# A new issue list for a fused attention and two mixture-of-experts kernel

## The chip, the core and the metric

The kernel runs on one core of a Trainium2 chip. Five instruction streams matter here: TensorE (PE in the profile, with its weight loads as PEld), VectorE (DVE), ScalarE (ACT), GpSimd (POOL) and SyncE (SP), which issues all DMAs. Each goes through its own list of instructions in order and waits on semaphores for what others produce. The metric is the device time of one execution in microseconds (us); lower is better.

## The reference

```python
# attention: batch 8, heads 8, seq 576, head_dim 64, 32 memory slots
a = softmax(phi, axis=seq)                    # per (b, h): 576 x 32
k_m = einsum('bhsm,bhsd->bhmd', a, k);  v_m = einsum('bhsm,bhsd->bhmd', a, v)
attn = softmax(q @ k_m.T / 8, axis=-1)        # 576 x 32
x = attn @ v_m                                # -> (4608 tokens, 512)
# first mixture: d_ff 768, the maximum of three products
h = maximum(maximum(x @ w1, x @ w2), x @ w3)
x = h @ w_out
# second, soft mixture: 8 experts with 4 slots each, F = 1024
logits = x @ phi2                             # 4608 x 32
d = softmax(logits, axis=0)                   # over all tokens
slot_in = d.T @ x                             # 32 x 512
for e in range(8):
    slot_out[e] = maximum(slot_in[e] @ W1[e], 0) @ W2[e]
c = softmax(logits, axis=1)
out = c @ slot_out
```

All of it is in fp32 in and out.

## The kernel before

The work is cut by batch entry n (8 of them, 576 tokens each) and, within it, by slices i (6 slices of 128 columns of the hidden 768). One pair (n, i) is a unit u; there are 48, and the first twelve mix n = 0 and n = 1. Since `x = attn @ v_m`, the product with `w1` to `w3` is folded: `v1` is `v_m` times the weights, and the expert matmuls multiply it by the attention matrix.

All of the main part up to a hand-over at the end is written as one string, `ORDER`: 1487 steps, separated by semicolons. A loop runs over it and calls the function that each step names (`for x in ORDER.split(";")`), so the order of steps in the string is the order of instructions on each engine. A step that stands later than another on the same engine never overtakes it. No scheduler moves anything afterwards. The code behind the loop, the tail, is written by hand: the last logits, the softmax over all tokens, the slots' experts (`ex_in`, L1016, takes the first weights), and the output.

The steps that the following speaks of, with the lines that the profile gives:

- `cva`, `cvb` (ACT), `cvd` (DVE, L318 and L319), `cvp` (POOL, L325) unpack weights; `raw`, `phit`, `phin`, `kv` and `q` are loads on SP. `send` (L286, L284) issues one piece of 512 KB of the second mixture's weights on SP, into a slot of memory that must be free. `late` opens further memory for these pieces (the tile `more`, and tiles that the earlier batch entries used).
- `warm` are filler matmuls (L801). `km`, `kvtm`, `scm`, `sct`, `s1r` to `s3t`, `s3h` and `s3l` (POOL, L532, writes `al`) make `k_m`, `v_m` and the attention matrix as a high part `ah` and a low part `al`.
- `v1m` (PE, L564), `v1h` (ACT, L573) and `v1l` (DVE, L579) make `v1` of a unit, in a high part `vh` and a low part `vl`.
- `mn u hf r` (PE, L597): six matmuls for unit u, half hf of its tokens and product r (0 to 2, for `w1` to `w3`), into one of three PSUM banks `m`. `ev u hf r` empties the bank: r = 0 is a copy on ACT (L607) into one of three buffers `g1`, r = 1 a maximum with it on DVE (L609), r = 2 the last maximum on DVE (L611) into the unit's tile `ht`. There are four `ht` buffers; a new unit's first L611 waits until all readers of the buffer's old unit are done.
- `ht` is read by `hrc` (POOL, L616), by `lg` (PE, L680, logits) and by a transpose. For n = 2 to 6, `trm` is a transpose on DVE (L643) into one of two half buffers and a DMA on SP out to memory (L645, `tr<-arena`); `trc` is a DMA on SP back in (L663, `hbuf<-tr`). For n = 7, `trm` is four transposes on PE (L639) and `trc` a copy on ACT (L659).
- `slm n k` (PE, L748) multiplies the transposed `hbuf` of three units by the softmax weights, after `ex`, `dtm` (PE, L733) and `dtc` (ACT, L737); `sla` (DVE, L760) adds it to the running sum.

The two steps at the heart, and the pools:

```python
ps_m = ctx.enter_context(tc.tile_pool(name="ps_m", bufs=3, space=PSUM))
gp = main_x.enter_context(tc.tile_pool(name="gp", bufs=3))
...
ht[n, i] = ring.tile([128, S], FP32, tag="ht", name="ht", bufs=4)
...
v = arena[:, o:o + 512]
nc.vector.transpose(out=v, in_=ht[n, i][:, 0:512])
...
nc.sync.dma_start(out=t, in_=v)
```

Of the kernel before, what the change touches and what calls it, by code (L numbers as in the profile page):

```python
# [22 lines left out]
for _x in (2, 3, 4, 5, 12, 6, 7, 13, 8, 9, 14, 15, 10, 11):  # L23
# [18 lines left out]
    "0 2; ev 1 1 0; raw 8; v1h 0 2; v1l 0 2; s1r 1 0; mn 1 0 0; cvp 7; ev 1 0 0; mn 1 0 2; cva 8; cvd 8; mn 1 0 "
    "1; ev 1 0 1; q 1 1; mn 2 0 0; raw 9; scm 1 1; ev 2 0 0; phi2; cvb 8; s1s 1 0; trm 0 0; trc 0 0; mn 2 1 0; ev "
    "1 0 2; s1e 1 0; sct 1 1; cvp 8; raw 11; mn 2 0 1; ev 2 1 0; hrc 0; mn 2 1 1; cva 9; cvb 9; raw 12; v1m 1 0; "
    "v1h 1 0; s2s 1 0; cvd 9; pt 0; pc 0; raw 10; ev 2 0 1; mn 2 0 2; ev 2 0 2; cvb 11; v1l 1 0; ev 2 1 1; mn 1 1 "
    "1; ev 1 1 1; mn 2 1 2; s2m 1 0; ev 2 1 2; phit 2; cva 11; cvp 9; raw 13; v1m 0 3; v1h 0 3; v1l 0 3; v1m 1 1; "
    "v1h 1 1; s3t 1 0; s3h 1 0; mn 1 1 2; ev 1 1 2; mn 4 0 0; ev 4 0 0; hrc 1; mn 4 1 0; ev 4 1 0; kv 2 0; cva "
    "10; mn 4 1 1; v1l 1 1; ev 4 1 1; mn 4 0 2; s1r 1 1; s3l 1 0; mn 3 0 0; ev 3 0 0; cvd 10; cvb 10; cvp 10; mn "
    "4 1 2; s1s 1 1; ev 4 1 2; cva 12; mn 4 0 1; ev 4 0 1; s1e 1 1; ev 4 0 2; pm 0; po 0; mn 5 0 0; s2s 1 1; mn 3 "
    "0 2; trm 0 1; hrc 4; trc 0 1; raw 14; cvd 11; cvp 11; pt 1; pc 1; mn 3 0 1; s2m 1 1; pt 2; pc 2; s3t 1 1; "  # L50
    "raw 15; s3h 1 1; s3l 1 1; ev 5 0 0; ev 3 0 1; ev 3 0 2; trm 0 2; phin 2; hrc 2; pm 1; po 1; cva 13; pm 2; lg "
    "0 0; cvb 12; cvd 12; cvp 12; lg 0 1; mn 3 1 0; ev 3 1 0; cva 14; mn 3 1 1; po 2; ev 3 1 1; cvb 14; mn 3 1 2; "
    "ev 3 1 2; hrc 3; cvb 13; mn 5 1 0; ev 5 1 0; trc 0 2; mxr 2; cvd 13; mn 5 1 1; trm 1 0; trc 1 0; mxd 2; mn 5 "
# [1127 lines left out]
```

## Time and profile before

| | |
|---|---|
| time, median of 3 runs (lowest to highest) | 465.71 us (465.19 to 467.65) |
| the profiled execution's own time | 465.06 us |
| its span in the trace | 463.3 us |
| mean granted clock of TensorE | 0.974 |
| busy, PE / DVE / ACT / POOL | 95% / 71% / 42% / 15% |

The time includes 1.8 us around the span. Busy is the share of the span in which an engine executes; a wait is the idle time in front of an instruction, put down to the one that released it. On a kernel whose PE is busy for 95%, it is PE's few idle stretches, and where they come from, that are worth reading.

### The profile page before, as it was taken

Reading aid. Unit: us, or ns where it says so; the run is one execution under the profiler, and the core shown is the slowest. Engines: PE = TensorE matmul, PEld = TensorE weight load, DVE = VectorE, ACT = ScalarE, POOL = GpSimd, SP = SyncE. Lnnn points to the kernel's source line nnn. Section 1 sums busy time; section 2 is a strip of 40 time slices with the busy share of each in tenths; the row PEclk is TensorE's granted clock in tenths of the full one; section 3 lists DMA queues with packets and bytes.
Section 4 is the critical chain, followed back from the end, with each engine's and each line's share of the span. In section 5 each row is a group of like instructions: output and inputs, shape, how many; then the busy total and the mean of one; then the engine's idle time right before and its main releaser. Section 6 shows DMA issues by size and latency. Waiting matters only on the chain.

```text
span 463.3 us, 12581 instructions
## 1 busy us (share of the span) xinstructions
PE 439.9 (95%) x5233; PEld 363.4 (78%) x5233; DVE 328.5 (71%) x753; ACT 192.6 (42%) x450; POOL 70.8 (15%) x92
## 2 busy tenths in 40 slices
PE   6999999999999999999999999998999989999981
PEld 5788899888997888888979879887878886654561
DVE  2397998767787968898679878999464434595541
ACT  3468768542544334243233433444333222133431
POOL 1137436421110011002100200112000000011000
PEclk9999999999999999999999999999999999999955
DMA  8967677558026137546368447779719905899988
GB/s 306 393 262 322 219 276 253 217 172 348 1 77 241 47 133 285 160 163 215 120 198 358 130 141 244 277 297 316 235 44 355 369 3 190 317 409 407 383 299 273
DMA packets 47657, 109.49 MB, mean 236 GB/s; under 512 B 3440, under 2 KB 26224, under 8 KB 45552
## 3 DMA queue, kind: packets, MB, share of 16 engines
q1 hardware_dynamic: 47600, 108.69, 64.8%
q8 instruction: 41, 0.67, 0.6%
q14 instruction: 16, 0.13, 0.1%
HBM read 91.38 MB, written 17.30 MB: 235 GB/s over the span
## 4 chain that ended last, share of the span: by engine, by line
PE 87%; DVE 4%; DMA 3%; ACT 2%; issue 1%; SPq 0%; DVEq 0%; ACTq 0%
PE m L597 49%; PE x L564 7%; PE l L801 5%; PE x L439 3%; PE x L1082 3%; PE x L748 2%; PE l L680 2%; PE x L475 2%; PE m L1016 2%; PE m L1033 2%; PE x L639 2%; DMA hbuf<-tr 2%; PE x L343 1%; PE l L1033 1%; DMA tr<-arena 1%
## 5 line engine op out<-in xcount | busy, mean ns | idle before, releaser
L597 PE MATMUL m<-ah,vh 128*128 128x288 f32 x576 | 171.2, 312 | 2.1 <-ACT g L607 1.5
L597 PE MATMUL m<-ah,vl 128*128 128x288 f32 x576 | 161.7, 296 | 0.0
L597 PEld LDWEIGHTS m<-ah,vh 128*128 128x128 f32 x576 | 108.3, 188 | 22.1 <-issue 9.4
L597 PE MATMUL m<-al,vh 128*128 128x288 f32 x576 | 123.3, 295 | 0.0
L597 PEld LDWEIGHTS m<-ah,vl 128*128 128x128 f32 x576 | 108.6, 188 | 0.2
L597 PEld LDWEIGHTS m<-al,vh 128*128 128x128 f32 x576 | 92.4, 188 | 0.1
L607 ACT ACTIVATE g<-m 128x288 f32<-128x288 f32 x96 | 38.9, 411 | 80.2 <-PE m L597 69.7
L609 DVE TENSOR_TENSOR g<-m,g 128x288 f32<-128x288 f32 x96 | 42.7, 450 | 33.0 <-PE m L597 22.4
L573 ACT ACTIVATE vh<-x 128x384 fp32r<-128x384 f32 (+1 forms) x100 | 42.0, 478 | 49.5 <-PE x L564 37.6
L611 DVE TENSOR_TENSOR ht<-m,g 128x288 f32<-128x288 f32 x96 | 42.7, 451 | 18.6 <-PE m L597 7.2
L579 DVE TENSOR_TENSOR vl<-x,vh 128x384 fp32r<-128x384 f32 (+1 forms) x100 | 48.8, 531 | 8.9 <-ACT vh L573 8.5
L532 POOL TENSOR_TENSOR al<-arena,ah 128x576 fp32r<-128x576 f32 x16 | 23.7, 1483 | 107.5 <-ACT ah L528 105.0
L564 PE MATMUL x<-arena,kvt 64*32 64x384 f32 (+1 forms) x800 | 39.3, 477 | 0.4 <-ACT vh L573 0.4
L325 POOL TENSOR_TENSOR arena<-arena 128x768 uint32<-128x768 uint32 (+1 forms) x13 | 23.4, 1804 | 39.5 <-ACT arena L313 14.5
L801 PE MATMUL l<-cst 128*128 128x128 f32 x162 | 25.3, 305 | 3.9 <-DMA cst<-in_consts_dram 3.2
L801 PEld LDWEIGHTS l<-cst 128*128 128x128 f32 x162 | 21.6, 208 | 7.3 <-DMA cst<-in_consts_dram 3.2
L564 PEld LDWEIGHTS x<-arena,kvt 64*32 64x32 f32 x800 | 12.0, 106 | 13.0 <-issue 8.1
L643 DVE STREAM_TRANSPOSE arena<-ht 128x512 f32<-128x512 f32 x30 | 20.7, 697 | 0.5 <-DMA tr<-arena 0.3
L439 PE MATMUL x<-arena 128*32 128x129 f32 x640 | 19.4, 274 | 0.2 <-ACT arena L402 0.2
L439 PEld LDWEIGHTS x<-arena 128*32 128x32 f32 x640 | 17.3, 110 | 2.9 <-ACT arena L402 0.9
L616 POOL COPY arena<-ht 128x64 f32<-128x64 f32 x24 | 5.2, 238 | 76.3 <-DVE ht L611 76.3
L528 ACT ACTIVATE ah<-arena 128x576 fp32r<-128x576 f32 x16 | 11.0, 684 | 11.2 <-DVE arena L518 11.2
(246 smaller groups left out, 587.3 us busy)
## 6 DMA issues: line engine op xcount, KB each, us to landing
arena<-in_e_w_dram SPq DMA_DIRECT2D x44, 512.0 KB, 7.5
arena<-in_w_dram SPq DMA_DIRECT2D x14, 768.0 KB, 6.0
arena<-in_kv_dram SPq DMA_DIRECT2D x8, 1290.0 KB, 9.5
arena<-in_q_dram SPq DMA_DIRECT2D x16, 576.0 KB, 7.0
arena<-in_kv_dram SPq DMA_DIRECT2D x8, 1032.0 KB, 8.1
tr<-arena SPq DMA_DIRECT2D x30, 256.0 KB, 3.0
hbuf<-tr SPq DMA_DIRECT2D x30, 256.0 KB, 4.3
arena<-in_phi_t_dram SPq DMA_DIRECT2D x8, 576.0 KB, 5.7
```

The costliest lines, as they stand in the source:

```text
L325: (eng or nc.gpsimd).tensor_tensor(out=du, in0=du, in1=lo.bitcast(U32), op=ALU.add)
L439: nc.tensor.matmul(t[32 * g:32 * g + 32, 0:KVC], phin_sb[:, j, b, 32 * g:32 * g + 32], kv_sb[:, j, b, g] if j < 4 else kv4_sb[:, g], start ...
L532: nc.gpsimd.tensor_tensor(out=al[n][:, :, c], in0=aT_sb[:, :, c], in1=ah[n][:, :, c].bitcast(FP32), op=ALU.subtract)
L564: nc.tensor.matmul(t[b][32 * g:32 * g + 32, 128 * r0:128 * r1], kvt[n][r, b, 32 * g:32 * g + 32], w_sb[r, i, r0:r1, g], start=True, stop=T ...
L573: nc.scalar.activation(out=v1[n, i][0][:, b, c], in_=ph["v1", n, i][b][:, c], func=ACTF.Copy)
L579: nc.vector.tensor_tensor(out=vl[:, b, c], in0=ph["v1", n, i][b][:, c], in1=vh[:, b, c].bitcast(FP32), op=ALU.subtract)
L597: nc.tensor.matmul(t[:, 0:HALF], x, y, start=(k == 0), stop=(k == 5))
L607: nc.scalar.activation(out=g1[u, hf], in_=t[:, 0:HALF], func=ACTF.Copy)
L609: nc.vector.tensor_tensor(out=g1[u, hf], in0=t[:, 0:HALF], in1=g1[u, hf], op=ALU.max)
L611: nc.vector.tensor_tensor(out=ht[n, i][:, cs], in0=t[:, 0:HALF], in1=g1.pop((u, hf)), op=ALU.max)
L643: nc.vector.transpose(out=v, in_=ht[n, i][:, 0:512])
L801: nc.tensor.matmul(t[:, 0:128], ident, ident, start=True, stop=True)
```

## The change

The string `ORDER` is replaced by another one. Its steps are the same ones, 1487 with the same arguments, the same 162 filler matmuls and the same 32 `send`; only their order differs, over its whole length. Nothing else in the kernel changes; the tail is the same code.

```diff
-    "dtc 6; slm 6 0; hrc 43; trc 7 4; sla 6 0; slm 6 1; sla 6 1; lg 7 1; ltm 0 3; hrc 40; trc 7 3; ev 47 1 2; ltc "
-    "0 3; lg 7 2; lg 7 3; lg 7 4; hrc 46; ev 47 0 2; hrc 47"
...
+    "1; hrc 46; mn 47 1 2; mn 47 0 2; ev 47 1 1; trm 7 2; trc 7 2; ltm 0 3; dtm 6; dtc 6; ev 47 0 2; trm 7 1; trc "
+    "6 3; trc 6 2; trm 7 4; trc 7 1; ev 47 1 2; trm 7 3; ltc 0 3; lg 7 1; slm 6 0; trc 7 3; slm 6 1; lg 7 2; lg 7 "
+    "3; trc 7 4; sla 6 0; sla 6 1; lg 7 4; hrc 47"
```

What that does to single engines is seen at three places. The first is SP's queue around the transfers that `slm 5 0` waits for. Here L645 is `tr<-arena` (out), L663 is `hbuf<-tr` (back in) and L286 a piece of weights. Before:

```order
L286 DMA arena<-in_e_w_dram 128x1024 x6
L645 DMA tr<-arena 128x512
L663 DMA hbuf<-tr 128x4x128
L645 DMA tr<-arena 128x512
L663 DMA hbuf<-tr 128x4x128
L286 DMA arena<-in_e_w_dram 128x1024 x3
L663 DMA hbuf<-tr 128x4x128 x3
L286 DMA arena<-in_e_w_dram 128x1024 x3
L645 DMA tr<-arena 128x512 x2
```

The two single L645 are `trm 5 5` and `trm 6 0`, and the five L663 in their order `trc 5 5`, `5 4`, `6 0`, `5 2` and `5 1`; three pieces stand directly ahead of the last three. In the new list:

```order
L286 DMA arena<-in_e_w_dram 128x1024 x4
L645 DMA tr<-arena 128x512 x2
L286 DMA arena<-in_e_w_dram 128x1024 x5
L645 DMA tr<-arena 128x512
L663 DMA hbuf<-tr 128x4x128 x3
L286 DMA arena<-in_e_w_dram 128x1024 x2
L645 DMA tr<-arena 128x512 x2
L286 DMA arena<-in_e_w_dram 128x1024 x3
```

In the new list `trc 5 2` and `trc 5 1` stand further up than these rows, and the three L663 here (`trc 5 4`, `5 0` and `5 5`) come directly behind the single L645 (`trm 6 0`) and ahead of the next pieces; `trc 5 0`, which stood further up before, is now the last that `slm 5 0` needs. The pieces stand in other groups as well.

The second place is ACT's last stretch ahead of the tail. L607 is `ev` with r = 0, L659 `trc` of n = 7, L737 `dtc 6`, and L794 `ltc`. Before:

```order
L573 ACTIVATE vh<-x 128x384 x2
L607 ACTIVATE g_5204<-m 128x288
L607 ACTIVATE g_5231<-m 128x288
L607 ACTIVATE g_5240<-m 128x288
L659 ACTIVATE hbuf<-x 128x4x4x32
L607 ACTIVATE g_5291<-m 128x288
L659 ACTIVATE hbuf<-x 128x4x4x32 x2
L607 ACTIVATE g_5356<-m 128x288
L737 ACTIVATE dk<-x 128x128
L659 ACTIVATE hbuf<-x 128x4x4x32 x2
L794 ACTIVATE hr_96<-x 128x384
```

In these rows L659 (`trc 7 0`, then `7 1` and `7 2`) stand between the L607; the last L607 comes behind three of them. In the new list:

```order
L573 ACTIVATE vh<-x 128x384 x2
L607 ACTIVATE g_5243<-m 128x288
L659 ACTIVATE hbuf<-x 128x4x4x32
L607 ACTIVATE g_5257<-m 128x288
L607 ACTIVATE g_5274<-m 128x288
L607 ACTIVATE g_5292<-m 128x288
L659 ACTIVATE hbuf<-x 128x4x4x32
L737 ACTIVATE dk<-x 128x128
L659 ACTIVATE hbuf<-x 128x4x4x32
L794 ACTIVATE hr_96<-x 128x384
L659 ACTIVATE hbuf<-x 128x4x4x32 x2
```

In the new list only `trc 7 0` stands among the L607; the other copies of n = 7 come behind the last of them.

The third place is DVE near unit 45 = (7, 3), in the same stretch. The numbers are those of buffers: a `ht` with a new number is a new unit's tile, L609 is `ev` with r = 1, L611 with r = 2. Before, `ht_5039` is unit 44 and `ht_5187` unit 45:

```order
L609 TENSOR_TENSOR g1_5059<-m_5173,g1_5059 128x288
L611 TENSOR_TENSOR ht_5039<-m_5154,g1_5059 128x288
L609 TENSOR_TENSOR g1_5188<-m_5196,g1_5188 128x288
L611 TENSOR_TENSOR ht_5187<-m_5206,g1_5188 128x288
L579 TENSOR_TENSOR vl_5193<-x_5122,vh_5192 128x384
L579 TENSOR_TENSOR vl_5193<-x_5123,vh_5192 128x384
L609 TENSOR_TENSOR g1_5240<-m_5251,g1_5240 128x288
L611 TENSOR_TENSOR ht_5187<-m_5213,g1_5240 128x288
```

In the new list `ht_4983` is unit 43, `ht_5155` unit 45 and `ht_5256` unit 46; `ht_4757` is unit 41 = (6, 5), and the L643 is its `trm 6 5`:

```order
L611 TENSOR_TENSOR ht_4983<-m_5180,g1_5078 128x288
L609 TENSOR_TENSOR g1_5172<-m_5190,g1_5172 128x288
L643 STREAM_TRANSPOSE arena_87<-ht_4757 128x512
L579 TENSOR_TENSOR vl_5210<-x_5082,vh_5209 128x384
L579 TENSOR_TENSOR vl_5210<-x_5083,vh_5209 128x384
L611 TENSOR_TENSOR ht_5155<-m_5215,g1_5172 128x288
L609 TENSOR_TENSOR g1_5156<-m_5223,g1_5156 128x288
L609 TENSOR_TENSOR g1_5257<-m_5235,g1_5257 128x288
L611 TENSOR_TENSOR ht_5155<-m_5260,g1_5156 128x288
L611 TENSOR_TENSOR ht_5256<-m_5277,g1_5257 128x288
```

In the list before, unit 45's tile takes the buffer of unit 42, which `trm 7 0` on PE reads. In the new list it takes the buffer of unit 41, which the L643 three rows ahead of its first L611 reads, and unit 46 takes that of unit 42.

## Rows read from the trace of the kernel before

**Rows 1.** page, part 1: busy us of each engine
```profile
PE 439.9 (95%) x5233; PEld 363.4 (78%) x5233; DVE 328.5 (71%) x753; ACT 192.6 (42%) x450; POOL 70.8 (15%) x92
```

**Rows 2.** windows: busy us of each engine, then granted clock, DMA share, GB/s
```profile
20.00:40.00 20.00, 19.41 (x226) 16.55 (x226) 18.45 (x38) 13.32 (x26) 8.62 (x6) 1.00 0.78 315
40.00:100.00 60.00, 59.75 (x672) 52.15 (x665) 50.34 (x102) 41.94 (x80) 30.05 (x22) 1.00 0.65 241
100.00:300.00 200.00, 199.93 (x2421) 171.36 (x2417) 163.92 (x375) 78.36 (x192) 19.58 (x37) 1.00 0.52 182
300.00:350.00 50.00, 48.27 (x577) 40.12 (x570) 36.16 (x85) 18.88 (x49) 5.47 (x9) 1.00 0.66 227
350.00:362.00 12.00, 12.00 (x116) 10.63 (x116) 5.51 (x14) 3.42 (x11) 0.65 (x3) 1.00 1.05 384
350.00:400.00 50.00, 47.11 (x489) 39.85 (x492) 22.23 (x56) 13.38 (x37) 1.72 (x8) 1.00 0.64 231
440.00:450.00 10.00, 8.39 (x71) 6.63 (x70) 4.59 (x13) 4.00 (x13) 0.00 (x0) 0.50 0.89 297
```

**Rows 3.** waits of PE, 300 to 390 us
```profile
PE x L748 <- DMA hbuf<-tr: 1.7, 1, 1.7
PE m L597 <- ACT g L607: 1.5, 2, 1.0
PE m L597 <- DVE ht L611: 0.6, 1, 0.6
```

**Rows 4.** chain that ended last, 312 to 325 us
```profile
312.45 3.29 DMA tr<-arena
...
317.19 7.58 DMA hbuf<-tr
...
324.86 0.85 PE x L748 x8
```

**Rows 5.** timeline of SP's queue, 313 to 318 us
```profile
313.72 1.36 SPq L286 DMA_DIRECT2D arena<-in_e_w_dram  x3
315.75 2.14 SPq L663 DMA_DIRECT2D hbuf<-tr  x3
```

**Rows 6.** page, part 6: DMA issues
```profile
hbuf<-tr SPq DMA_DIRECT2D x30, 256.0 KB, 4.3
```

**Rows 7.** timeline of DVE near 372 us
```profile
372.13 0.46 DVE L611 TENSOR_TENSOR ht<-m,g 128x288 f32<-128x288 f32 x1 [3.85 <-PE x L639]
```

**Rows 8.** timeline of PE, 371 and 383 us
```profile
371.50 0.60 PE L639 MATMUL x<-cst,ht 128*128 128x128 f32 x4
...
383.06 0.29 PE L597 MATMUL m<-ah,vh 128*128 128x288 f32 x1
...
383.85 0.27 PE L733 MATMUL x<-cst,dt 128*128 128x128 f32 x1
```

**Rows 9.** timeline of ACT, 381 us
```profile
381.20 0.60 ACT L659 ACTIVATE hbuf<-x 128x512 f32<-128x512 f32 x1 [0.63 <-PE x L639]
381.70 0.41 ACT L607 ACTIVATE g<-m 128x288 f32<-128x288 f32 x1
```

**Rows 10.** line L532 by itself: ns min/median/max
```profile
L532 POOL TENSOR_TENSOR al<-arena,ah x16: 1414/1437/2238, 31.6 to 322.3; 128x576 fp32r<-128x576 f32 x16
```

**Rows 11.** timeline of PE and SP, tail's start
```profile
399.69 1.07 PE L1016 MATMUL m<-extra,p 128*32 128x256 f32 x16
...
400.39 0.80 SPq L286 DMA_DIRECT2D extra<-in_e_w_dram  x2
```

**Rows 12.** timeline of SP's queue, 346 to 363 us
```profile
346.60 0.80 SPq L286 DMA_DIRECT2D more<-in_e_w_dram  x2
...
350.45 2.23 SPq L286 DMA_DIRECT2D arena<-in_e_w_dram  x3
...
355.51 0.93 SPq L645 DMA_DIRECT2D tr<-arena  x2
...
362.42 0.93 SPq L663 DMA_DIRECT2D hbuf<-tr  x2
```

253 rows, old and new, of the table ORDER are left out of this document.

## Prediction

> **What bounds the kernel now.** I read the page's busy times first. TensorE (PE) is busy 439.9 of 463.3 us, VectorE (DVE) 328.5 [rows 1], so the question is where PE stands idle and whether a new order can take that idle time away. The windows answer where [rows 2]: between 100 and 300 us PE is busy 199.93 of 200.00 us, between 40 and 100 us 59.75 of 60.00. There is nothing to win there, only something to lose. It is idle 0.59 us between 20 and 40 us, 1.73 us between 300 and 350, and 2.89 us between 350 and 400. The list that is searched anew ends at the hand-over to the tail, about 399 us; the code behind it stays.
>
> The waits of PE between 300 and 390 us come next [rows 3]. Three kinds are all there is: one wait of 1.7 us of a slot matmul (L748) for a transfer into `hbuf`, two waits of the expert matmuls (L597) for ACT's eviction `ev` with r=0 (L607), 1.5 us together, and one of 0.6 us for DVE's eviction with r=2 (L611). Together 3.8 us. These are the terms of the sum if the new order removes them.
>
> Where each comes from:
>
> The 1.7 us. The chain of waits [rows 4] goes from `tr<-arena`, issued at 312.45 and landed 3.29 us later, to a transfer `hbuf<-tr` issued at 317.19 that takes 7.58 us, and then to the eight matmuls of `slm 5 0` at 324.86. SP's timeline [rows 5] says why it took that long: three weight pieces (L286) are issued from 313.72, and only behind them, from 315.75, the three `hbuf<-tr`, of which the last is the one that `slm 5 0` needs. The median of this transfer is 4.3 us [rows 6], so 3.3 us of the 7.58 are crowding.
>
> The 0.6 us. DVE's timeline [rows 7] has an L611 at 372.13 after 3.85 us of waiting for a PE transpose (L639). It is `ev 45 1 2`; the buffer `ht` of unit 45 is that of unit 42, which `trm 7 0` reads, and PE comes to `trm 7 0` only at 371.50 [rows 8]. Until DVE goes on, PE's next matmul has no free `m` bank.
>
> The 1.5 us. ACT's timeline [rows 9] shows the larger of the two: an L607 at 381.70 (`ev 46 0 0`) stands behind a copy of PE's transposes (L659, `trc 7 2`) that waited 0.63 us for PE until 381.20. ACT goes through its list in order, so an eviction that was ready waits for a copy that nobody needs yet, and PE waits for the bank.
>
> **The change, part by part.** The steps are the same 1487, so no work is added or removed. Each engine's own list is all that changes, and each term is a wait.
>
> Slot matmul: `trc 5 2` and `trc 5 1` stand far earlier on SP, and `trc 5 0`, now the last that `slm 5 0` needs, comes directly behind `trm 6 0` and ahead of the next pieces. The three pieces that stood ahead were a wait of 2.0 us (313.72 to 315.75 [rows 5]), and the crowding was 3.3 us; five pieces ahead of `trm 6 0` may crowd in their place, but that stands some 5 us earlier against `slm 5 0` by the PE steps between. To lose the whole of 1.7 it is enough that the last transfer is issued 1.7 us earlier. I take the whole: -1.7 (bounds -1.7 and 0).
>
> ACT's copies: in the new order all L607 stand ahead of `trc 7 1` to `7 4`, only `trc 7 0` among them, so the pattern of [rows 9] is gone: -1.5 (bounds -1.5 and -0.5, if one of the two returns behind `trc 7 0`).
>
> DVE's buffer: unit 45's `ht` now reuses the buffer of unit 41, which is freed by DVE's own transpose `trm 6 5` (L643) directly ahead of it, and `trm 7 0` stands earlier on PE for the next unit: -0.6 (bounds -0.6 and 0).
>
> What may be given back at the end: evictions, transposes and copies are packed into the same stretch. DVE is busy 22.23 of 50 us and ACT 13.38 of 50 between 350 and 400 us [rows 2], so throughput is not short, only single orders. I take +0.3, a fifth of the 1.5 us that two such waits cost (bounds 0 and +1.0, the longest of them [rows 3]).
>
> Start, to 65 us: PE idles 0.59 + 0.25 us there [rows 2], so -0.8 is the most to gain. Against it, DVE is busy 18.45 of 20.00 us between 20 and 40 us with 38 instructions, 0.49 us each, and 50.34 of 60.00 behind that; two of them moved ahead of an eviction that PE needs cost 1.0 us. The new list swaps neighbours there and puts `mn 1 1 1` ahead of `mn 1 1 0`, so that its bank is held until both are evicted; counted step by step DVE's work and PE's come out level, 7.7 us each. I take 0 (bounds -0.8 and +1.0).
>
> A page speaks on one neighbour in that stretch. The row: `s3l 0 1` on GpSimd (POOL, L532) took 2238 ns where the median of 16 is 1437 [rows 10], 0.8 us more, and it lay across a DVE instruction with two SBUF inputs (L319). The Trainium skill, SBUF — State Buffer, section Who interferes with whom, says that such a DVE instruction and a GpSimd instruction that reads SBUF exclude each other for a whole instruction, whichever came first. The trace agrees with 0.8 us in one case of 16. By that rule the new order, in which `s3l 0 1` falls beside other DVE steps, could be up to 0.8 us better or worse for `al`; PE did not wait for it before, so the sum has 0 either way.
>
> Middle, 65 to 300 us: bounds 0 and +1.0 (one wait as long as the longest ACT wait at the end [rows 3]); the likeliest places are a DVE step that waits for a `phin` load, and a late `s3l`. I take 0.
>
> The tail: its first step, `ex_in(0)` (L1016), starts at 399.69, and the stream of weight pieces that fills the DMA queues follows at 400.39 [rows 11]. It hangs on buffers that PE's last steps free, so what the list saves shifts the whole tail.
>
> Sum, against the profiled execution's 465.06 us: 465.06 - 1.7 - 1.5 - 0.6 + 0.3 = 461.6. That execution lies 0.65 us below the median of the three runs (465.71), inside their spread of 465.19 to 467.65; by the median the sum is 462.2. I say **461.8**. With the bounds on all terms: 460.5 (-0.8 at the start, nothing given back) to 465 (below).
>
> **The rivals.** 0.5% is 2.33 us, about what a measurement of this kernel tells from no change: 463.38 to 468.04.
>
> (a) *The wait moves to `slm 6 0`.* The new order transposes `trm 6 5` late on DVE, behind `mn 45 0 1`, and issues its `tr<-arena` and then five `hbuf<-tr` in a row. Between `mn 45 0 1` and `slm 6 0` PE has 15 expert steps of 0.79 us (383.06 to 383.85) and five transposes of 0.60 us [rows 8], 14.9 us. DVE's eviction and transpose take about 1.4 us of it, 13.5 remain. The transfers need at best 3.3 us [rows 4], four issues of 0.7 us (2.14 for three [rows 5]), and 4.3 us [rows 6], 10.5 us; at worst 6.9 us, as `tr<-arena` issued from 355.51 was waited for until 362.42 [rows 12], 2.9 and 7.6 [rows 4], 17.4 us. So from 3.0 us of margin to 3.9 us of stall. Three weight pieces stand ahead of these transfers in the queue and none behind, so I hold the good half for likelier. With the stall, or with several of the bounds above at once (+1.0, +1.0, +0.7): 463.5 to 465.2.
>
> (b) *Slower: SP's queue stops DVE.* Once the list has opened more memory for weights, the new order issues ten pieces ahead of the `tr<-arena` of `trm 6 4` and `trm 6 3`, where before it was seven. Before, the first went out at 346.60, SP had to wait within the last three (2.23 us), and the two `tr<-arena` behind them, issued from 355.51, were waited for until 362.42 [rows 12], 15.8 us after the opening: the queues are full there, 1.05 busy at 384 GB/s [rows 2], so a piece of 512 KB takes 1.4 us. Now the opening comes 1.7 us earlier, at 344.9, three pieces more cost 4.2 us and two `hbuf<-tr` of half that size fewer give back 1.4: landed near 344.9 + 15.8 + 2.8 = 363.5. `trm 6 5` writes the half buffer that `trm 6 3`'s transfer reads, and it stands on DVE ahead of `v1l 7 4` and of evictions of units 45 to 47: if the transfer is late, DVE stands, no bank comes free and PE stands, 1:1. DVE wants it behind `mn 45 0 1`, 20 expert steps after the opening (15.8 us at 0.79 [rows 8]) and four `v1m` and three `lg`, some 3.5 us by my estimate: 364.7 with its eviction. The margin is 1.2 us, and 2.5 if a step takes 0.85 as it does behind a change of step; there it decides. To end 0.5% above before, the transfer would have to be 8 us later than counted: 468.1 or more. No transfer of this stretch shows such a delay, which speaks against it; a small overrun belongs to (a).
>
> (c) *The gain is hidden in the tail.* If the weight stream at 400.39 [rows 11] hung on something other than PE's last steps, the end would stay where it is and the list's gain would turn into waits for weights: 465.1. For it speaks that DMA is full in such stretches (1.05 [rows 2]); against it, that SP issues nothing new between 398 and 400 us and begins right behind L1016's start.
>
> (d) *More than the waits.* In the last part PE runs at half its clock: a granted clock of 0.50 between 440 and 450 us, 1.2 GHz, with 8.39 us of 10 busy, where it was 1.00 up to 400 [rows 2]. If the shifted tail kept the full clock longer, the queue of outputs, 0.89 busy there, would be the bound: about 1.1 us in these 10, 460.5 or a little less. Nothing in the tail's own order changes, which speaks against it.
>
> **The numbers.** Forecast 0.60 (own range 460.5 to 463.3), (a) 0.17, (c) 0.08, (b) 0.11, (d) 0.04. Faster by over 0.5%: the forecast and (d), 0.64. Within: (a) and (c), 0.25. Slower: (b), 0.11, which includes mishaps of that size that I did not find in a list of 1487 steps. The range leaves out (b) and the lower half of (d): 460.0 to 465.4.
>
> **What would show it.** Right: no PE wait over 0.3 us for `hbuf<-tr` at `slm 5 0`; no wait of L597 for L607 or L611 behind 365 us; `ex_in(0)` near 396.2 and the tail as long as before, 63.6 us from there to the span's end. Wrong: a PE wait at L748 near 380 (a), a DVE L643 with a long wait for `tr<-arena` near 365 (b), new PE waits between 40 and 300, or a longer tail with waits for weights (c).

## The result, and the profile after

The changed kernel takes 461.02 us (median of 4 runs, 459.66 to 462.82) against 465.67 for the kernel before (4 runs): the ratio is 0.9914, with a 95% interval of 0.9885 to 0.9942. The prediction was 461.8, in a range of 460.0 to 465.4. Run again in more rounds (e1 below) the ratio is 0.9878 (0.9848 to 0.9908). The ratios are those of the record, and not the quotients of the medians beside them (here 0.9900). One execution of e7 (469.45 us) was in a slower state and is left out of the table below. So the kernel is faster by about 1%, and the number was right. Its parts were not all right.

The profiled execution of the changed kernel is its slowest one: 462.82 us with a span of 461.0. Against the execution of before, 465.06, that is only 2.24 us less; the other 2.4 us are the distance of both traces from their medians (0.61 and 1.80). Its page, part 1, answers to [rows 1]:

```profile
PE 439.0 (95%) x5233; PEld 363.8 (79%) x5233; DVE 333.3 (72%) x753; ACT 192.4 (42%) x450; POOL 71.4 (15%) x92
```

And its windows (busy us of each engine, then granted clock, DMA share, GB/s) to [rows 2]:

```profile
20.00:40.00 20.00, 18.50 (x202) 16.24 (x186) 17.95 (x38) 12.47 (x24) 8.18 (x5) 1.00 0.89 348
40.00:100.00 60.00, 59.43 (x690) 51.00 (x692) 52.30 (x100) 42.14 (x81) 30.81 (x21) 1.00 0.55 209
100.00:300.00 200.00, 198.68 (x2345) 171.56 (x2334) 162.82 (x369) 77.56 (x191) 17.86 (x35) 1.00 0.54 186
300.00:350.00 50.00, 50.00 (x636) 41.07 (x634) 38.83 (x90) 19.74 (x51) 7.38 (x12) 1.00 0.59 203
350.00:400.00 50.00, 49.15 (x544) 42.10 (x544) 24.06 (x62) 13.88 (x38) 1.78 (x8) 1.00 0.77 282
```

Between 300 and 350 us PE now has no idle time, and between 350 and 400, where the tail begins 2.7 us earlier, 0.85 us. That is what was forecast. But between 20 and 40 us it is idle 1.50 us where it was 0.59, between 40 and 100 us 0.57 instead of 0.25, and between 100 and 300 us 1.32 instead of 0.07. The view of PE's waits names them (total us, times, longest):

```profile
PE x L564 <- DVE vl L579: 0.8, 1, 0.8
PE x L439 <- DMA arena<-in_kv_dram: 0.7, 1, 0.7
PE m L597 <- DVE ht L611: 0.6, 1, 0.6
PE m L597 <- ACT g L607: 0.5, 1, 0.5
PE x L564 <- ACT vh L573: 0.4, 1, 0.4
```

Two of these are of the kinds of [rows 3], but at other places. Between 300 and 390 us, where [rows 3] are from, the same view has none of the three: the waits for `hbuf<-tr`, for L607 and for L611 at the end are gone. New ones, 2.6 us together, stand at 29.71 (L579), 67.33 (L607), 132.18 (L611) and 260.29 us (a load of `kv`); the one of 0.4 us is the old list's too.

How the sum comes out: the list before comes to `slm 5 0` at 324.86 [rows 4] after a wait of 1.74, so without it at 323.1. The new list comes to it at 325.84 without a wait, with steps done that take PE 0.5 us more (`v1m 6 5` and an expert step, against an expert step and `rtm 0 1`). It has lost 2.2 us up to there. The first L1016 stands at 397.00, where it was 399.69 [rows 11]: from `slm 5 0` on, 71.16 us instead of 74.83, less the 0.5, a gain of 3.2 us. So the hand-over moves by 2.2 - 1.74 - 3.2 = -2.7 us, which is the -2.69 that the two rows give.

### The profile page after: what moved, and what is told of

Same layout as the page of the kernel before. It is cut to its first block, busy times and chain, and to the rows that moved or that the text cites. A ratio compares the mean times of both kernels' runs of the same rounds, so it can differ in the third digit from the quotient of the medians.

```text
span 461.0 us, 12577 instructions
## 1 busy us (share of the span) xinstructions
PE 439.0 (95%) x5233; PEld 363.8 (79%) x5233; DVE 333.3 (72%) x753; ACT 192.4 (42%) x450; POOL 71.4 (15%) x92
## 4 chain that ended last, share of the span: by engine, by line
PE 85%; DVE 5%; DMA 3%; issue 2%; ACT 2%; SPq 1%; POOL 1%; DVEq 0%; ACTq 0%; POOLq 0%
PE m L597 48%; PE x L564 7%; PE l L801 4%; PE x L439 3%; PE x L1082 3%; PE x L748 2%; DMA arena<-in_kv_dram 2%; PE x L475 2%; PE l L680 2%; PE m L1033 2%; PE m L1016 2%; PE x L639 2%; PE x L343 1%; PE l L1033 1%; SPq L663 1%
## 5 line engine op out<-in xcount | busy, mean ns | idle before, releaser
L597 PE MATMUL m<-ah,vh 128*128 128x288 f32 x576 | 171.4, 312 | 1.2 <-DVE ht L611 0.6
L597 PE MATMUL m<-ah,vl 128*128 128x288 f32 x576 | 161.8, 295 | 0.0
L597 PEld LDWEIGHTS m<-ah,vh 128*128 128x128 f32 x576 | 108.2, 188 | 20.6 <-issue 12.4
L597 PE MATMUL m<-al,vh 128*128 128x288 f32 x576 | 123.2, 295 | 0.1
L597 PEld LDWEIGHTS m<-ah,vl 128*128 128x128 f32 x576 | 108.4, 188 | 0.4
L597 PEld LDWEIGHTS m<-al,vh 128*128 128x128 f32 x576 | 92.3, 188 | 0.3 <-POOL al L532 0.3
L607 ACT ACTIVATE g<-m 128x288 f32<-128x288 f32 x96 | 38.9, 410 | 70.8 <-PE m L597 62.5
L609 DVE TENSOR_TENSOR g<-m,g 128x288 f32<-128x288 f32 x96 | 42.5, 449 | 31.0 <-PE m L597 24.4
L611 DVE TENSOR_TENSOR ht<-m,g 128x288 f32<-128x288 f32 x96 | 42.4, 450 | 20.3 <-PE m L597 9.0
L579 DVE TENSOR_TENSOR vl<-x,vh 128x384 fp32r<-128x384 f32 (+1 forms) x100 | 48.7, 530 | 3.3 <-ACT vh L573 2.8
L564 PE MATMUL x<-arena,kvt 64*32 64x384 f32 (+1 forms) x800 | 39.5, 477 | 1.3 <-DVE vl L579 0.8
L532 POOL TENSOR_TENSOR al<-arena,ah 128x576 fp32r<-128x576 f32 x16 | 23.3, 1465 | 72.1 <-ACT ah L528 42.5
L325 POOL TENSOR_TENSOR arena<-arena 128x768 uint32<-128x768 uint32 (+1 forms) x13 | 23.5, 1808 | 34.5 <-ACT arena L313 24.2
L801 PE MATMUL l<-cst 128*128 128x128 f32 x162 | 25.0, 303 | 3.8 <-DMA cst<-in_consts_dram 3.2
L801 PEld LDWEIGHTS l<-cst 128*128 128x128 f32 x162 | 21.6, 208 | 7.1 <-DMA cst<-in_consts_dram 3.2
L616 POOL COPY arena<-ht 128x64 f32<-128x64 f32 x24 | 6.3, 279 | 124.5 <-DVE ht L611 98.9
L564 PEld LDWEIGHTS x<-arena,kvt 64*32 64x32 f32 x800 | 12.4, 105 | 13.5 <-issue 7.8
L439 PE MATMUL x<-arena 128*32 128x129 f32 x640 | 19.8, 274 | 1.1 <-DMA arena<-in_kv_dram 0.7
L643 DVE STREAM_TRANSPOSE arena<-ht 128x512 f32<-128x512 f32 x30 | 20.5, 697 | 0.2
L439 PEld LDWEIGHTS x<-arena 128*32 128x32 f32 x640 | 17.3, 110 | 3.2 <-DMA arena<-in_kv_dram 0.9
L481 DVE STREAM_TRANSPOSE arena<-x 128x288 f32<-128x288 f32 x32 | 13.3, 457 | 3.7 <-PE x L475 3.7
```

Source lines behind the costliest of these rows:

```text
L325: (eng or nc.gpsimd).tensor_tensor(out=du, in0=du, in1=lo.bitcast(U32), op=ALU.add)
L439: nc.tensor.matmul(t[32 * g:32 * g + 32, 0:KVC], phin_sb[:, j, b, 32 * g:32 * g + 32], kv_sb[:, j, b, g] if j < 4 else kv4_sb[:, g], start ...
L532: nc.gpsimd.tensor_tensor(out=al[n][:, :, c], in0=aT_sb[:, :, c], in1=ah[n][:, :, c].bitcast(FP32), op=ALU.subtract)
L564: nc.tensor.matmul(t[b][32 * g:32 * g + 32, 128 * r0:128 * r1], kvt[n][r, b, 32 * g:32 * g + 32], w_sb[r, i, r0:r1, g], start=True, stop=T ...
L579: nc.vector.tensor_tensor(out=vl[:, b, c], in0=ph["v1", n, i][b][:, c], in1=vh[:, b, c].bitcast(FP32), op=ALU.subtract)
L597: nc.tensor.matmul(t[:, 0:HALF], x, y, start=(k == 0), stop=(k == 5))
```

## The experiments

The times, each beside the kernel before on the same chip, and the place of the first L1016 in the trace of each:

| kernel | us | before, us | ratio (95%) | L1016 at |
|---|---|---|---|---|
| e1 changed, again | 461.00 | 467.20 | 0.9878 (0.9848 to 0.9908) | 396.22 |
| e2 new from step 880 | 458.81 | 467.20 | 0.9839 (0.9804 to 0.9873) | 394.07 |
| e3 old from step 880 | 468.49 | 467.20 | 1.0033 (1.0004 to 1.0062) | 404.05 |
| e4 old to step 150 | 459.49 | 467.20 | 0.9864 (0.9824 to 0.9905) | 394.74 |
| e5 before, again, one run | 464.90 | 466.88 | | 400.81 |
| e6 SP's edit only | 464.54 | 466.88 | 0.9962 (0.9928 to 0.9996) | 403.29 |
| e7 the end by hand | 462.00 | 466.88 | 0.9907 (0.9876 to 0.9938) | 398.58 |
| e8 filler ahead of the wait | 459.83 | 466.88 | 0.9842 (0.9804 to 0.9880) | 394.51 |
| e9 three pieces ahead | 471.04 | 466.85 | 1.0097 (1.0071 to 1.0124) | 405.85 |
| e10 five steps by hand | 461.12 | 466.85 | 0.9871 (0.9845 to 0.9898) | 395.07 |
| e11 transpose early | 462.83 | 468.14 | 0.9897 (0.9856 to 0.9938) | 397.81 |
| e12 filler in e2 | 460.26 | 468.14 | 0.9863 (0.9813 to 0.9912) | 394.87 |

**e1, the changed kernel once more**, nothing edited.

> The changed kernel once more, nothing edited. Its first trace lost 1.7 us of PE time between 20 and 65 us against the kernel before, got back 2.0 us at slm 5 0 and 3.1 us behind 365 us. Theory A (the list costs time at the start): the waits at v1m (0.85 us near 29.7), at L597 near 67 us and 132 us come again at the same places, and the hand-over (first L1016) comes again near 397.0. Rival B (that trace was an unlucky execution): these waits are gone or elsewhere and the hand-over comes near 395.5. The time is 461.0 by either, ratio 0.990.

The waits of 0.42 and 0.85 us at the start, the one near 132 us and the one for `kv` (0.5) came again; the one near 67 us did not. The hand-over stands at 396.22, between what the two theories said. So the start's loss belongs to the list (A), and 0.8 us of the first trace were that execution's own.

**e2, e3 and e4, the two lists cut and joined.** Up to their steps 880 (before) and 879 (new) the two lists have done the same steps but one, near 230 us, and again nearly so near step 150. Each kernel takes one list to such a point and the other's order of what is left:

```diff
 # e2: ORDER[before][:880] + what is left, in the new order      (before's start and middle)
 # e3: ORDER[new][:879]    + what is left, in the order before   (new start and middle)
 # e4: ORDER[before][:150] + what is left, in the new order      (before's start)
```

> The list of before up to its step 880 (mxr 7, near 235 us), and from there the new list's order of what is left. Theory A: the start and the middle of before are kept, the gains of 2.0 and 3.1 us behind it are had, and the time is some 5 us below before and 1.5 to 2 us below the new list: 460.5 to 459.2. Rival B (start losses are not the list's): the same time as the new list, 461.0. Rival C (the end's gain needs what the new list did before): waits come back at slm 5 0 or behind 365 us, 463 or more.

> The other half: the new list up to the same point, and from there the order of before. Theory A: the three waits of before are back (1.7 at slm 5 0, 1.5 and 0.6 behind 365 us), and the start's loss of about 1.7 us comes on top: 467. Rival B: no loss at the start, the time of before, 465.7.

> The list of before up to its step 150 only (near 47 us), the new list's order from there. Theory A: if the loss is in the first 47 us, this wins it back and goes 1.0 to 1.7 us below the new list, 459.3 to 460.0; if it is between 47 and 65 us, where DVE's order decides, it stays at 461.0. Rival B: 461.0 in any case.

Theory A held in all three. e2 is the fastest kernel of the study, 2.2 us below e1 on the same chip; e3 is slower than the kernel before, by 0.3%; and e4, which takes only the first 150 steps from the old list, wins 1.5 us over e1 by the medians, so half or more of the loss lies ahead of 47 us. More cannot be said from e4: two of its six executions (462.3 and 462.5) lie above all of e1's, and its traced one was early already at the first L439 (14.84 us, and 15.26 in e2, which has the same steps up to there). Its trace has no wait of L564 for L579 (`v1l`) any more. In e3 the wait at `slm 5 0` is back, and longer, as its view of PE's waits shows:

```profile
PE x L748 <- DMA hbuf<-tr: 2.6, 1, 2.6
```

And in this trace the wait costs more than itself. It ends at 327.72, and from 329.1 to 332.5 us the granted clock is 0.50, as this window shows (the clock is the third figure from the end):

```profile
329.00:332.50 3.50, 3.50 (x28) 3.00 (x13) 1.02 (x2) 1.28 (x3) 0.00 (x0) 0.51 0.65 253
```

From `slm 5 0` to the first L1016 are 76.33 us, 1.5 more than in the first trace of before (74.83), which has the same order there and a clock of 1.00. In e5, below, a longer wait at the same place is not followed by a fall; what decides it, no run shows.

**e5, the kernel before once more**, one run.

> The kernel before once more, to see what its slower executions (up to 469 us, against 465.06 in the first trace) are made of. Theory: the wait at slm 5 0 hangs on when DMA data lands and is longer in them (2 to 4 us instead of 1.7), and the waits behind 365 us (0.50, 0.55, 0.99) are the same to 0.02 us. Rival: the time is lost in the tail, where the half clock and the weights decide; then the first L1016 stands near 399.7 again.

Its waits of PE between 300 and 390 us:

```profile
PE x L748 <- DMA hbuf<-tr: 3.2, 1, 3.2
PE m L597 <- ACT g L607: 1.5, 2, 1.0
PE m L597 <- DVE ht L611: 0.6, 1, 0.6
```

With the very same list the wait at `slm 5 0` is 3.2 us instead of 1.7, and those behind 365 us are the same to 0.01 us (0.50, 0.55, 0.99). So the wait that hangs on when data lands differs between executions, and the three that hang on the order of an engine's steps do not. The four traces that have this wait give 1.74, 3.22, 2.64 (e3) and 2.02 us (e7): the first was the shortest, and a prediction made against it expects too little of this term.

What the longer executions of before are made of, e5 does not show. They spread from 464.53 to 470.57 us on that chip, but the traced one was short: 464.90 us, with the longer wait and a hand-over 1.1 us later than in the first trace, since its tail took 62.3 us instead of 63.6. So the theory about them is not tested.

**e6, SP's part of the change alone.**

```diff
-  ...; hrc 32; rl 0 6; trc 5 2; trc 5 1; slm 5 0; ...
+  ...; mn 37 1 2; trc 5 2; trc 5 1; send 1; send 1; send 1; ...; hrc 32; rl 0 6; slm 5 0; ...
```

> The kernel before with one edit: trc 5 2 and trc 5 1 stand ahead of the three pieces (behind mn 37 1 2) instead of behind them. Theory: the wait of 1.7 us at slm 5 0 goes and the hand-over comes 1.7 to 2.0 us earlier, with the three waits behind 365 us unchanged: ratio 0.996. Rival: the pieces then come late or crowd a later transfer and the time is given back at slm 5 1 or slm 6 0: ratio 1.0.

The time fits the theory, the trace fits the rival. `slm 5 0` at 326.38 no longer waits, but 11 us later there is a wait in its place. In the timeline of DVE:

```profile
335.80 0.71 DVE L643 STREAM_TRANSPOSE arena<-ht 128x512 f32<-128x512 f32 x1 [2.57 <-DMA tr<-arena]
```

In that of PE:

```profile
337.47 0.30 PE L733 MATMUL x<-cst,dt 96*128 96x96 f32 x1 [1.69 <-ACT dt L719]
```

`trm 6 3` (L643) waits 2.57 us for the `tr<-arena` that reads its half buffer; DVE's steps for the softmax weights stand behind it, and PE waits 1.69 us for them. That transfer (of `trm 6 1`, the second of a pair on SP behind three pieces) is issued at 328.26, 1.9 us behind `slm 5 0`; in the list before it was issued at 324.60, 0.3 us ahead of it, while PE waited. The one wait had hidden the next. What is left of the gain, 0.4%, I put down to those executions in which that wait was longer than 1.7 us; that is argued from e5 and e3, not shown.

This traced execution also began 3.2 us late: the first L439 starts at 18.74 us instead of 15.55. It is not the first load, which landed 0.1 us later. The same fillers (L801) and transposes (L397) took about twice as long, as the chain shows, first before and then in e6:

```profile
9.72 1.17 PE l L801 x8
...
11.87 0.87 PE x L397 x8
```

```profile
10.15 2.09 PE l L801 x8
...
13.93 1.71 PE x L397 x8
```

The trace's first record of the granted clock, 1.00 (2.4 GHz), stands at 16.1 us in e6 and at 9.0 us in before; in the other traces it stands between 7.1 and 9.6 us. (The windows print 1.00 ahead of the first record too.)

**e7, the end by hand.** Two steps of the list before are moved.

```diff
-  ...; mn 45 1 2; mn 45 0 2; ...; v1l 7 4; trm 7 0; trc 7 0; ...
+  ...; mn 45 1 2; trm 7 0; mn 45 0 2; ...; v1l 7 4; trc 7 0; ...
-  ...; mn 46 0 1; trm 7 1; trc 7 1; mn 46 0 2; ...; trm 7 3; ev 46 0 0; ...
+  ...; mn 46 0 1; trm 7 1; ev 46 0 0; trc 7 1; mn 46 0 2; ...; trm 7 3; ...
```

> The kernel before with two edits at the end: trm 7 0 on PE directly behind mn 45 1 2 (for the ht buffer of unit 45), and ev 46 0 0 on ACT ahead of trc 7 1 and trc 7 2. Theory: both L607 waits (1.5 us) and the L611 wait (0.6 us) go, 2 to 3 us: ratio 0.994 to 0.996; the wait at slm 5 0 stays. Rival: ACT's or DVE's wait only moves on to the next eviction (unit 47), and half or less is won.

The theory held for the trace. From L748's start at 326.60 to L1016 at 398.58 are 71.98 us, 2.85 less than in the list before, and none of the three waits is left. Two steps out of 1487 bring most of what the new list brings at the end (3.2). It also shows that 2.04 us of idle time, by the rows, cost 2.85 us. A likely reason, not shown, is that a busy PE in these rows is not PE at its peak, as the profile's page says of its modelled ends. The ratio, 0.9907, is better than the 0.994 to 0.996 that were expected; where the rest of it comes from, the one trace does not show.

**e8, the start of the changed kernel.** One filler is moved.

```diff
-  ...; v1m 0 0 2 3; s3h 0 0; v1h 0 0 2 3; warm 8; warm 11; ...
+  ...; warm 8; v1m 0 0 2 3; s3h 0 0; v1h 0 0 2 3; warm 11; ...
```

> The changed kernel with one edit: the filler warm 8 stands ahead of v1m 0 0 2 3 instead of behind it. Theory: the new list lost 0.85 us near 29.7 us because PE waits there for v1l 0 0 1 2 with no filler ahead; with the filler ahead the wait goes and everything behind comes 0.85 us earlier, 460.2 against 461.0. Rival: DVE is the bound there, and the time comes back as waits behind 35 us: 461.0.

Its waits of PE between 20 and 300 us:

```profile
PE m L597 <- DVE ht L611: 0.6, 1, 0.6
PE x L564 <- ACT vh L573: 0.4, 1, 0.4
PE x L439 <- DMA arena<-in_kv_dram: 0.4, 1, 0.4
```

The wait for L579 (`v1l`) is gone, nothing came in its place, and the hand-over is 1.7 us earlier than in e1. Of these, 0.2 us were there ahead of the moved filler, and 1.2 arise at it (the first L597 stands at 33.47 us instead of 34.90); all six executions are below all of e1's, on another chip. PE's filler is work that has to be done in any case; behind the wait it is added to it, ahead of it it covers it.

**e9, three pieces ahead of `trm 6 4`** on SP.

```diff
-  ...; trm 6 4; ...; v1m 7 4; send 1; v1m 7 5; send 1; ...; send 1; ...
+  ...; send 1; send 1; send 1; trm 6 4; ...; v1m 7 4; v1m 7 5; ...
```

> The changed kernel with the three pieces that follow trc 6 4 put ahead of trm 6 4 and trm 6 3 on SP's queue (3 x 1.28 us). Theory (rival b of the prediction as a mechanism): in the new list tr<-arena of trm 6 3 landed 2.0 us before DVE wanted its half buffer for trm 6 5; with 3.8 us more DVE's L643 waits some 1.8 us, evictions stand behind it, and PE loses 1 to 1.8 us: 462 to 463 against 461.0. Rival: the banks and buffers in hand cover it: 461.0.

It does not test what it was meant to test. Pieces go into memory from which `v1m 7 4` and `v1m 7 5` still read their weights, and these steps now read pieces of another matrix: that part of the computation is changed. PE waits for a piece to land, as its timeline shows:

```profile
366.00 1.53 PE L564 MATMUL x<-arena,kvt 64*32 64x384 f32 x16 [8.30 <-DMA arena<-in_e_w_dram]
```

8.3 of the 10 us are this wait, not DVE's. For the rival it says nothing.

**e10, five steps by hand**: e6 and e7 together, and `trm 6 3` moved behind `rdc`, so that the wait that e6 showed goes too.

```diff
-  ...; ev 39 1 2; trm 6 3; mn 40 0 0; ...; rtm 1 0; rdc; rsm 0; ...
+  ...; ev 39 1 2; mn 40 0 0; ...; rtm 1 0; rdc; trm 6 3; rsm 0; ...
```

> The kernel before with all edits by hand: trc 5 2 and 5 1 ahead of the three pieces, trm 6 3 behind rdc (the wait that appeared in its place), trm 7 0 behind mn 45 1 2, ev 46 0 0 ahead of trc 7 1. Theory: five moved steps hold the new list's whole gain, without its start: 5 us below before and below the changed kernel by 1 to 2 us, 459 to 460 against 461.0. Rival: the searched list's many other moves are needed and a part of the waits comes back: 462 or more.

None of the three waits is left, nor the one of e6, and L1016 stands at 395.07, 1.15 us ahead of e1. The time is the changed kernel's, not 1 to 2 us less: its tail took 63.93 us in that trace (62.78 in e1), since its last two groups of L1033 took 1.18 and 2.02 us where the others took 1.00: the weights' stream, of which more is said below. Five moved steps hold what the new list gained; that they are better than it is not shown.

**e11, the transpose early**: the rival (b) as a mechanism.

```diff
-  ...; ev 45 0 0; v1l 7 5; ev 43 0 2; ...; mn 45 0 1; ev 45 0 1; trm 6 5; trc 6 5; ...
+  ...; ev 45 0 0; trm 6 5; trc 6 5; v1l 7 5; ev 43 0 2; ...; mn 45 0 1; ev 45 0 1; ...
```

> The changed kernel with trm 6 5 (and its trc 6 5) ahead of v1l 7 5 on DVE, four evictions earlier. Theory (rival b as a mechanism, with a dependence that the three pieces of the run before did not keep): in e1 the tr<-arena of trm 6 3 landed at 365.84 and DVE would now want the half buffer at 363.8, so its L643 waits 2.1 us, v1l 7 5 and four evictions stand behind it, and PE waits 1 to 2 us for banks near 366: 462 to 463 against 461.0. Rival: three banks and DVE's idle time of 1.5 us behind cover it: 461.0.

In DVE's timeline:

```profile
365.33 0.71 DVE L643 STREAM_TRANSPOSE arena<-ht 128x512 f32<-128x512 f32 x1 [1.85 <-DMA tr<-arena]
```

In PE's:

```profile
367.37 0.40 PE L597 MATMUL m<-ah,vh 128*128 128x288 f32 x1 [1.68 <-DVE ht L611]
```

The theory held to 0.3 us: DVE waits 1.85 us for `tr<-arena`, PE 1.68 for the eviction that stands behind, and the kernel takes 462.83 (e1: 461.00, on another chip; L1016 1.59 us later, and 1.9 us counted from `slm 5 0`). The mechanism of the rival is real; in the new list it was not reached.

**e12, the rule of e8 put into e2.**

```diff
-  ...; v1m 0 0 2 3; v1h 0 0 2 3; phit 1; s1s 0 0; cvd 1; s1r 0 1; s1e 0 0; warm 4; ...
+  ...; warm 4; v1m 0 0 2 3; v1h 0 0 2 3; phit 1; s1s 0 0; cvd 1; s1r 0 1; s1e 0 0; ...
```

> e2 (before up to step 880, the new order from there) with the filler warm 4 ahead of v1m 0 0 2 3 in the part of before, where PE waited 0.42 us for ACT. Theory: the best of both lists and the start's rule of e8: 0.4 us below e2, 458.4, 1.9% below before. Rival: no difference from e2, 458.8.

Its waits of PE between 20 and 100 us:

```profile
PE m L597 <- POOL al L532: 0.7, 1, 0.7
PE m L597 <- ACT ah L528: 0.7, 1, 0.7
```

A miss. The wait of 0.4 us for ACT goes, but ACT's `s3h` and POOL's `s3l` come 2.2 us later than in e2, and the first expert steps wait 0.7 us for each of them. 460.26 is no gain over e2. A part of the 2.2 us is the moved filler: `v1h 0 0 2 3` and the steps behind it on ACT and DVE come about half a us later. The larger part is one DVE instruction, `s2m 0 0` (L514), which takes 2.40 us where the other 15 take 0.75. DVE's timeline:

```profile
29.15 2.40 DVE L514 TENSOR_TENSOR arena<-arena,ssum 128x576 f32<-128x576 f32 x1
```

POOL's:

```profile
28.78 2.16 POOL L325 TENSOR_TENSOR arena<-arena 128x768 uint32<-128x768 uint32 x1 [2.73 <-ACT arena L313]
```

L514 has two SBUF inputs and started 0.4 us behind POOL's L325. In e2 it ran at 28.60, and POOL's L325 began behind it, at 29.44. So e12 does not refute the rule of e8; it shows that a moved filler also changes which instructions of DVE and POOL meet. `s3h` waits for DVE's L518, which stands behind L514.

## Why the prediction was right, and where not

The number is in part luck. Up to `slm 5 0` the new list lost 2.2 us where the sum has 0, and behind it it won 3.2 us where the sum has 1.8, so two errors cancel in part. What was right is which waits go, and in the main why.

*The three waits go.* Right in all: behind 300 us no row of them is left. The terms were -1.7, -1.5 and -0.6, with +0.3 given back. Mis-sized are two. The end measured -3.2 (e7: -2.85 with two steps) instead of -1.8: nothing was given back, and in e7 the waits cost PE more than their idle rows say. The slot matmul is -1.7 in the traced pair, but 3.2 in e5.

*The reading of [rows 5].* The three pieces are not all that held back the three `hbuf<-tr`. SP had issued the pieces by 315.08 (313.72 + 1.36). The first of the three L663 is `trc 6 0`, which needs the `tr<-arena` of `trm 6 0`, landed at 315.74 (312.45 + 3.29 [rows 4]), and the queue went on at 315.75; the pieces crowd these transfers. In e5 that `tr<-arena` landed at 318.58, the three went out from 318.60, and PE waited 3.2 us. e6 moved the two L663 ahead of the pieces and of `trc 6 0` alike, so it does not part the two causes.

*ACT's and DVE's places.* In the new trace's timeline of ACT the evictions L607 stand ahead of the copies L659 as in the order shown, and each waits for PE, not PE for it:

```profile
374.47 0.41 ACT L607 ACTIVATE g<-m 128x288 f32<-128x288 f32 x1 [1.19 <-PE m L597]
376.04 0.41 ACT L607 ACTIVATE g<-m 128x288 f32<-128x288 f32 x1 [1.17 <-PE m L597]
381.35 0.60 ACT L659 ACTIVATE hbuf<-x 128x512 f32<-128x512 f32 x1 [4.90 <-PE x L639]
```

In DVE's timeline `trm 6 5` and the first L611 of unit 45 start without a wait:

```profile
368.89 0.70 DVE L643 STREAM_TRANSPOSE arena<-ht 128x512 f32<-128x512 f32 x1
...
370.43 0.44 DVE L611 TENSOR_TENSOR ht<-m,g 128x288 f32<-128x288 f32 x1
```

*`slm 5 0` has 5 us.* Wrong in the margin. SP's timeline of the changed kernel:

```profile
318.16 0.33 SPq L645 DMA_DIRECT2D tr<-arena  x1
318.54 1.57 SPq L663 DMA_DIRECT2D hbuf<-tr  x3
```

And PE's:

```profile
325.84 0.51 PE L748 MATMUL x<-hbuf,dk 128*32 128x384 f32 x1
```

`trc 5 0` is issued 0.5 us behind the first L663, 319.0, and landed at 324.2; the last of the three, landed at 325.0, is `trc 5 5`, which `slm 5 0` does not need. PE came at 325.84. So the transfer took 5.2 us where the median is 4.3 [rows 6]: it was crowded, as the prediction allowed, and 1.6 us were left.

*Start: 0, bounds -0.8 and +1.0.* This step failed. "Counted step by step DVE's work and PE's come out level": between 45 and 65 us neither trace of the new list has a wait, but the loss lies ahead of that, at a place that the count passed over. PE's `v1m 0 0 2 3` stands ahead of its filler in the new list and waits for DVE there. e4 gives 1.5 us for the first 150 steps by the medians, and 1.1 by the hand-over without that early start (396.22 - 394.74 - 0.42); in e8 1.2 us arise at the one filler. So the term was at its upper bound or somewhat beyond, where 0 was taken.

*Middle: 0, bounds 0 and +1.0.* At its upper bound or beyond: one wait of 0.57 near 132 us and one of 0.5 to 0.7 for a load of `kv` came in both traces, 1.1 to 1.2 us together, and in the first one of 0.5 near 67 us besides. Neither of the two places that were named (a `phin` load, a late `s3l`) was among them.

*Rival (a), `slm 6 0`.* Said: from 3.0 us of margin to 3.9 of stall. SP's timeline:

```profile
366.28 0.37 SPq L663 DMA_DIRECT2D hbuf<-tr  x1
...
374.98 2.58 SPq L663 DMA_DIRECT2D hbuf<-tr  x5
```

And PE's:

```profile
383.27 1.47 PE L748 MATMUL x<-hbuf,dk 128*32 128x384 f32 x16
```

Five `hbuf<-tr` are issued from 374.98, the last landed at 382.24, and `slm 6 0` starts at 383.27 without a wait: a margin of 1.0 us.

*Rival (b), SP's queue.* Said: `tr<-arena` landed near 363.5, a margin of 1.2 to 2.5 us. The L663 that waits for the first of the two goes out at 366.28 (above), the second landed at 366.9, and DVE's L643 started without a wait at 368.89: 2.0 us. The times on the clock came about 3 us later than counted, most of it the 2.2 us lost ahead of 326; the margin was right, and e11 shows what lies behind it.

*Rival (d), the clock.* The clock did stay high longer in some traces of the new list, but e5 shows that the list need not be the cause. The window from 438 to 440 us of the changed kernel, with the granted clock third from the end:

```profile
438.00:440.00 2.00, 1.46 (x13) 1.15 (x13) 1.07 (x4) 0.97 (x4) 0.00 (x0) 0.68 0.48 167
```

The same window of e2:

```profile
438.00:440.00 2.00, 1.73 (x18) 1.44 (x21) 0.76 (x2) 0.66 (x2) 0.00 (x0) 0.51 1.00 327
```

The same window of e5, the list before:

```profile
438.00:440.00 2.00, 1.60 (x16) 1.02 (x15) 1.05 (x3) 1.04 (x3) 0.00 (x0) 1.00 1.09 386
```

In the output stage the clock stays at 0.50, 1.2 GHz, from its first fall to the end. In before and after it fell at nearly the same time, 439.0 and 438.7, although the output stage (the last L1058) began at 436.30 and 434.52; e1 and e2 began at 432.93 and 431.09 and fell at 438.7 and 438.1. From that L1058 to the start of PE's last group of matmuls are 17.24, 16.95, 16.49 and 16.38 us. In these four whoever came earlier did more of the output at 2.4 GHz, and it looks as if up to 0.9 us were won on top of the waits. But e5 shows that the same list can do it too: the list before, with the latest of these hand-overs, kept the clock to 444.2, 6.8 us into the stage, and took 16.38 us. And in e8 the clock fell at 434.6, 3.1 us into the stage, which took 17.0 us. TensorE: Matmul & The Clock Gate, a page of the Trainium skill, in its section What's actually happening, has two states of the clock by how busy PE has been; the trace agrees in that PE was busy 2.00 of 2 us between 432 and 434 and 1.55 of 2 between 436 and 438, ahead of the fall. What sets the time of the fall, no run here shows.

*The rule on SBUF's ports that the prediction takes from the Trainium skill, SBUF — State Buffer, section Who interferes with whom.* The trace agrees once more, at another place, which POOL's timeline shows. The `s3l 0 1` that was 0.8 us longer before [rows 10] is the first row, and now stands alone:

```profile
42.60 1.46 POOL L532 TENSOR_TENSOR al<-arena,ah 128x576 fp32r<-128x576 f32 x1 [5.60 <-ACT ah L528]
...
73.44 1.92 POOL L532 TENSOR_TENSOR al<-arena,ah 128x576 fp32r<-128x576 f32 x1 [3.77 <-ACT ah L528]
```

DVE's timeline has beside the second:

```profile
73.12 0.96 DVE L319 SCALAR_TENSOR_TENSOR arena<-arena,lt 128x768 uint32<-128x768 uint32 x1
```

The one at 73.44 meets this L319, which has two SBUF inputs and was there first, and takes 1.92 us instead of 1.44: 0.48 more, where L319 still had 0.6 us to run. PE waited for neither. In e12 it was POOL that came first, DVE's L514 that lost 1.65 us, and PE that waited.

*(c), the gain hidden in the tail.* Not as put: the stream of weights follows the hand-over. But it has no slack. In the first trace of the changed kernel one step of the chain that ended last is nearly twice as long as its neighbours:

```profile
430.03 1.00 PE m L1033 x16
...
431.58 1.93 PE m L1033 x15
```

The pieces landed every 1.28 us, with one gap of 2.72 us (415.97 to 418.69), and the last matmuls waited for the last piece at 432.85. Before, its last piece landed at 434.60, in time. This cost 0.9 us, half of the 1.8 by which that execution lay above its median.

*The signs.* Those for right came: no wait at `slm 5 0`, none of L597 for L607 or L611 behind 365 us, the first L1016 at 397.0 and 396.2 (e1) where 396.2 was said, and a tail of 64.0 and 62.8 us where 63.6 was. But two of those for wrong came too: new waits of PE between 40 and 300 us, and in the first trace a tail that waited for weights.

## What to carry to other kernels

In a kernel that keeps one engine busy for 95%, read the few waits by what they hang on: the waits of 0.5 to 1 us on another engine's order at the end came back to 0.01 us (one of half a us near 67 us did not), and a few moved steps removed them, while a wait on data that lands differed by 1.5 us, so that one trace does not give its size. Look behind each wait for the next one that it hides, as the transpose behind `slm 5 0`. Where filler is part of the list, put it ahead of an instruction that waits, and look in the new trace at what now meets: e8 won by it, and e12 lost by one DVE instruction that ran into POOL's. And compare a late time with another execution of the same list before a cause in the list is named: the clock's rise at the start and its fall at the end changed the time by up to 3.2 and 0.9 us.

## What was not expected of the hardware

The granted clock fell to 0.50 between 2.6 and 7.0 us after the start of the output stage, in traces of nearly the same tail, two of them of the very same list (2.7 and 6.8). In one execution (e6) PE's first matmuls ran at half their rate to 16 us instead of 9, which put all that follows 3.2 us later. In another (e3) a wait of 2.64 us in mid-kernel was followed by 3.4 us at half the clock; in e5 a wait of 3.22 us at the same place was not. And 2.04 us of idle rows were 2.85 us of time.
